# Attention and two MLPs on one core: the put-off product's matrices loaded two at a time into the token tile, and token loads, output stores and two late MLP1 products placed elsewhere

## The chip, the cores and the metric

The kernel runs on one NeuronCore of a Trainium2 chip. Its engines are TensorE (PE in the rows, its weight loads PEld), VectorE (DVE), ScalarE (ACT), GpSimd (POOL) and SyncE (SP), which here does nothing but issue DMAs. The metric is device time in microseconds of one execution; lower is better. The time of a kernel is the median of its runs, and a verdict of faster or slower is given beyond 2%.

## The reference

```python
def reference(...):                       # 4 x 8 heads, 768 positions, head size 64
    for c in range(24):                   # chunks of 32 queries
        # keys: 8 memory keys + positions c*32-16 .. c*32+40
        scores = q_c @ k_full.T / 8
        attn_out[c] = softmax(scores) @ v_full
    x = attn_out as 3072 tokens x 512
    h = x @ moe_w_in;  x = (h * sigmoid(h)) @ moe_w_out       # MLP1, 512 -> 2048 -> 512
    h = x @ moe2_w_in; r = max(h, 0); out = (r * r) @ moe2_w_out   # MLP2, same sizes
```

Everything is float32. The kernel splits an operand of a product into a high part and a remainder (`fp32r` tiles) and makes three matmuls for one.

## The kernel before, in words

**Stages.** Attention and MLP1 run first, in 6 blocks of 512 tokens. MLP1 (`mlp`, L745) takes 16 hidden tiles of a block: 12 matmuls of 128x512 into a hidden tile (L756 to L758), activation and split on ACT and DVE, then 12 matmuls (L790 to L792) that add the hidden tile's part to four output tiles `acc`. The result y1 is stored in DRAM (L831, L836). From about 612 us on MLP2 runs alone (`second`, L1203).

**MLP2.** Its two matrix products are made by a scheme of 2x2 blocks with 7 products in place of 8 (as Winograd's), on sums of blocks, called forms here. There are 6 blocks of 512 tokens, and in each 8 pairs of hidden tiles (k0 to k7). For a pair PE makes 7 "visits" (`visit`, L942: the sums of the tokens times the forms of the first weight matrix, tile `pp`) and 6 back products (`back_out`, `multiply` L1071: the squared hidden sums g times the forms of the second weight matrix, tile `out`). The back products lag: those of pair n stand among the visits of pairs n+1 and n+2. One such product is six matmuls of 128x256. The seventh back product of each pair is **put off**: its left operand stays in a `kept` tile, and the block's eight put-off products (`fourth`, here F0 to F7) are made among the visits of pairs k1 and k2 of the next block, those of the last block at the end. In a block there are so 8 x 13 + 8 = 112 products.

**What is loaded.** All forms of the second matrix (`w2s` in DRAM) are loaded anew in every block, by DMAs that SP issues at L1016: per pair one of 512 KB for back products 0 and 1 (here "f0"), two of 256 KB for 2 and 3 ("f2", "f3"), one of 512 KB for 4 and 5 ("f4"). The 512 KB ones use a ring of two buffers `wraw`, the 256 KB ones a ring of four buffers `wu`, which also take the eight 256 KB loads of the put-off products' forms (`load_fourth`). A load into a ring waits until PE is done with the buffer's last user. `tokens` (L849) reads a block's y1 back by four loads of 256 KB into a tile `xf` (L863), makes four differences of them (L875, on DVE or POOL), and splits seven forms (high part L900 on ACT, remainder L904 on DVE or POOL). xf and the last four splits live in a ring of two buffers "x", which MLP1 used before. Here a **border** is the stretch in which the next block's first pairs run: pair k0, and k1 and k2 with F0 to F7.

**Behind the put-off products.** `combine` adds the block's sums; three of its four output quarters are complete before F7 and are stored by `store` (L1180); `finish` adds the fourth and stores it.

**Order.** Each operation is a `Piece` with engines and costs, a due time and what it must follow. `Graph.order` plays the costs through on a model clock: an engine that is free takes the ready piece with the earliest due time. What comes out is each engine's program, which the chip then runs in that order; an engine that waits holds up all that stands behind it. SP's program is one such order, its DMAs go to one hardware queue, and at most eight are open at a time, since eight semaphores rotate. PE's products of MLP2 are chained in the order of the code (`on_tensor`).

Of the kernel before, what the change touches and what calls it, by code (L numbers as in the profile page):

```python
# [14 lines left out]
F32R = mybir.dt.float32r  # L15
# [173 lines left out]
def chunk_attention_two_mlps(ctx, tc, units, weights, out):  # L189
# [14 lines left out]
    for tag, n in (  # L204
        ("raw", 3), ("pr", 1), ("pts", 1), ("xq", 3), ("x", 2), ("g", 3), ("wraw", 2),
        ("wu", 4), ("wr", 4), ("nm", 3), ("sm", 4),
    ):
        pool(tag, n)
# [6 lines left out]
    def f(ap):  # L215
        return ap.bitcast(F32)
# [14 lines left out]

    ones, dense = G.buf("x"), G.buf("ph")

# [226 lines left out]
    def split_x(j, p, po, done, due):  # L460

        new = []
        if j not in x_buf:
            x_buf[j] = G.buf("x")
            x_done[j] = []
            new = [x_buf[j]]
        xb = x_buf[j]

        def x_high(e):
            if new:  # L470
                take(xb, [P, 2, KT, TB], F32R)
            nc.scalar.copy(xb.tile[:, 0, p, :], po.tile)

        def x_low(e):
            t = xb.tile
            nc.vector.tensor_tensor(t[:, 1, p, :], po.tile, f(t[:, 0, p, :]), op=ALU.subtract)

        a = G.add({"ACT": 0.64}, due - 1, x_high, [*done, *x_done[j]], new=new, uses=[po, xb])
        x_done[j].append(G.add({"DVE": 0.7}, due, x_low, [a], uses=[po, xb],
                               port=j >= ON_PE))  # L480
# [264 lines left out]
    def mlp(j):  # L745
        accs, earlier = None, []
        size = step_due(j, 1) - step_due(j, 0)
        for i in range(FT):
            ph, g, due = G.buf("ph"), G.buf("g"), step_due(j, i)
            wb, xb = w_buf[i], x_buf[j]  # L750
# [32 lines left out]
            def back(e, i=i, wb=wb, g=g, some=range(KT)):  # L783
                w, t = wb.tile, g.tile
                first, last = i == 0, i == FT - 1
                for m in some:
                    acc = accs[m]
                    o = take(acc, [P, TB], F32) if first else acc.tile
                    ws = slice(DM + m * P, DM + (m + 1) * P)
                    nc.tensor.matmul(o, w[:, 1, ws], t[:, 0], start=first, stop=False)  # L790
                    nc.tensor.matmul(o, w[:, 0, ws], t[:, 1], start=False, stop=False)  # L791
                    nc.tensor.matmul(o, w[:, 0, ws], t[:, 0], start=False, stop=last)  # L792

            if j == NB - 1 and i == FT - 1:
                break
            y = G.add({"PE": 2.8}, due + 2.4 * size, back, [d, w_done[i, 1]],
# [12 lines left out]

        def part(at, m):  # L810
            ys.append(on_tensor(MM, at, lambda e: back(e, some=[m]), [d, w_done[FT - 1, 1]], [],
                                [wb, g, accs[m]]))
            if m == KT - 1:
                store(ys)

        return y, [lambda at, m=m: part(at, m) for m in range(KT)]

# [31 lines left out]
    def tokens(b, due):  # L849

        t0 = b * T2
        after, xf = stored[b], G.buf("x")
        loads = []
# [4 lines left out]
        for n, (k, half) in enumerate(((0, 0), (2, 0), (2, 1), (0, 1))):  # L858
            def load(e, n=n, k=k, half=half):
                if n == 0:  # L860
                    take(xf, [P, 7, 2, HALF2], F32, "xf")
                at = t0 + half * HALF2
                nc.sync.dma_start(  # L863
                    out=xf.tile[:, n],
                    in_=y1[k:k + 2, :, at:at + HALF2].rearrange("k p t -> p k t"),
                )

            p = G.add({"SP": 0.45}, due - 50 + n, load, after, new=[xf] * (n == 0),
                      uses=[xf] * (n > 0), size=P * T2 * 4)
            p.behind += loads[:1]  # L870
            loads.append(p)

        def sums(o, a, b, after, at):
            def emit(e):
                engine[e].tensor_tensor(form(o), form(a), form(b), op=ALU.subtract)  # L875

            return G.add({"DVE": 0.72, "POOL": 1.35}, at, emit, after, uses=[xf], port=True)

# [8 lines left out]
        for rank, n in enumerate(X_FORM[p] for p in PRODUCTS):  # L887
# [3 lines left out]
            if shared:  # L891
                four = four or [G.buf("x")]
                x = four[0]
            else:
                x = G.buf("raw")
# [203 lines left out]

    def load_fourth(some, tag, due):  # L1100
        k, m = some[0].k, len(some)
        w, d = load_out(w2s[k:k + m, NF - 1], m, tag, due, [x for q in some for x in w2_kept[q.k]])
        for i, q in enumerate(some):
            q.fourth = (w, i, d)

    def load_pair(q, due, past=()):

        load_some(q, 0, 2, "wraw", due - 10)
        for k in range(4 if past else 0):
            load_fourth(past[k:k + 1], "wu", due - 11 + k)  # L1110
        for j in (2, 3):
            load_some(q, j, 1, "wu", due - 9 + j + (2 if past else 0))
        if past:
            for k in range(4, PAIRS):
                load_fourth(past[k:k + 1], "wu", due - 8 + k)
        load_some(q, 4, 2, "wraw", due - 5)
# [26 lines left out]
    def combine(b, due):  # L1143
# [24 lines left out]
        d12 = add(u2, 3, u2, [a4], 3)  # L1168
        store(b, y22, 1, 1, d22, due + 3)
        store(b, t1, 0, 0, d11, due + 4)  # L1170
        store(b, u2, 0, 1, d12, due + 5)
        return u3, [a4, d22]

    def store(b, y, half, side, after, due, m=None):
        r0, cs = b * T2 + half * HALF2, slice(side * HALF2, (side + 1) * HALF2)

        def emit(e):
# [3 lines left out]
            else:  # L1181
                nc.sync.dma_start(out=out[r0 + m * P:r0 + (m + 1) * P, cs], in_=y.tile[:, m])

        G.add({"SP": 0.45}, due, emit, [after], uses=[y],
              size=P * HALF2 * 4 * (2 if m is None else 1))

    def finish(b, u3, after, due):

        bank = banks[b, 4]
        for m, one in enumerate(bank):  # L1190
            def emit(e, m=m, one=one):
                if len(bank) == 1:
                    nc.vector.tensor_tensor(u3.tile, one.tile, u3.tile, op=ALU.add)
                else:
# [4 lines left out]
                      uses=[one, u3])  # L1199
            store(b, u3, 1, 0, d, due, None if len(bank) == 1 else m)  # L1200

    pairs = {}

    def second(rest):
        t, steps, xs, result = T20, NB2 * PAIRS, {}, {}
        half = PAIRS // 2
        for n in range(steps):
            q = pairs[n] = Pair(n)
            if q.k == 0:
                xs[q.b] = tokens(q.b, t)  # L1210
            one, two = pairs.get(n - 1), pairs.get(n - 2)
            past = [pairs[(q.b - 1) * PAIRS + k] for k in range(PAIRS)] if q.b else []
            if one:
                load_pair(one, t + 8 * MM, past if q.k == 1 else ())

# [12 lines left out]
            slots = [[x for x in some if not isinstance(x, tuple) or x[0]] for some in slots]  # L1228
            if n == 0:
                for i, x in enumerate(rest):  # L1230
                    slots[i].append(x)
            due, at = [], t
# [23 lines left out]
        past = [pairs[b * PAIRS + k] for k in range(PAIRS)]  # L1256
        for k in range(half):
            load_fourth(past[k:k + 1], "wu", t - 8 + MM * k)
        load_pair(one, t + 7 * MM)
        for k in range(half, PAIRS):  # L1260
            load_fourth(past[k:k + 1], "wu", t + MM * k)
        for k in range(half // 2, half):
# [7 lines left out]
        for j in range(NF - 1):  # L1270
            back_out(one, j, t)
            t += MM
        u3, after = combine(b, t)
        for x in past[half:]:
            fourth(x, t, True)
            t += MM
        finish(b, u3, after, t)

# [89 lines left out]
```

## Time and profile before

| | us |
|---|---|
| median of 3 runs | 1117.77 (1114.66 to 1492.04) |
| profiled execution | 1117.68 |
| its span, first to last instruction | 1115.8 |
| PE busy in the span | 1089.7 (98%) |
| DVE, ACT, POOL busy | 806.9, 517.3, 182.0 |

The profiled execution is an ordinary one: its time is that of the median. PE's busy time includes matmuls that run at the lower clock level and those that are drawn out behind a pause, so what the kernel could win is more than the idle 2%. The page's row of PE clocks has full speed (9 tenths or more) in 39 of 40 slices; slices are 28 us wide.

### The profile page before, as it was taken

To read this page: it belongs to the slowest core of one execution; us is meant where nothing else is said; L and a number is where in the kernel's file an instruction comes from. 1 tells how busy PE (TensorE), PEld (TensorE's weight loads), DVE (VectorE), ACT (ScalarE), POOL (GpSimd) and SP (SyncE) were. 2 spreads that over 40 slices of the span, in tenths; PEclk is the share of its full clock that TensorE was granted. 3 is DMA by queue.
4 is the path that set the end of the run, shared out by engine and by line. 5 is a ranking of instruction groups with operands and counts; after the bars stand their busy time and mean duration, and the time that the engine had idled before them with its cause. 6 is when DMAs were issued, how large, how long until landed. Compare 5 with 4: busy or idle time off the path is not lost.

```text
span 1115.8 us, 23506 instructions
## 1 busy us (share of the span) xinstructions
PE 1089.7 (98%) x9484; PEld 957.5 (86%) x9484; DVE 806.9 (72%) x1818; ACT 517.3 (46%) x926; POOL 182.0 (16%) x171
## 2 busy tenths in 40 slices
PE   7999999999999999999999999999999999999998
PEld 5677777777777777777888999899999999999997
DVE  4777777768778767775687767767767768768666
ACT  2888643544434444542566335334334335335332
POOL 0032202202101200110001202302302302303000
PEclk6999999999999999999999999999999999999999
DMA  7875344343334432431343556756756766755756
GB/s 267 274 231 181 105 139 163 117 143 114 118 129 157 149 123 96 143 128 39 120 134 127 158 170 190 245 171 181 255 171 199 244 171 206 244 164 174 234 170 206
DMA packets 94587, 188.36 MB, mean 169 GB/s; under 512 B 8464, under 2 KB 20752, under 8 KB 94480
## 3 DMA queue, kind: packets, MB, share of 16 engines
q1 hardware_dynamic: 94480, 186.88, 52.2%
q8 instruction: 74, 1.21, 0.5%
q14 instruction: 33, 0.27, 0.1%
HBM read 159.58 MB, written 27.26 MB: 167 GB/s over the span
## 4 chain that ended last, share of the span: by engine, by line
PE 92%; DMA 5%; issue 1%; SPq 1%; POOL 0%; DVE 0%; ACT 0%; POOLq 0%
PE pp L942 20%; PE out L1071 20%; PE ph L756 9%; PE ph L758 8%; PE acc L790 8%; PE ph L757 8%; PE acc L792 8%; PE acc L791 8%; DMA w<-w2s 3%; PE po L417 2%; PE sc L331 2%; DMA xf<-y 1%; PE turned L382 1%; DMA raw<-units 1%; DMA w<-weights 1%
## 5 line engine op out<-in xcount | busy, mean ns | idle before, releaser
L1071 PE MATMUL out<-w,g 128*128 128x256 f32 x2016 | 275.6, 284 | 11.5 <-DMA w<-w2s 10.4
L942 PE MATMUL pp<-xs,forms 128*128 128x256 f32 x2016 | 272.3, 281 | 0.5 <-ACT sums L959 0.5
L1071 PEld LDWEIGHTS out<-w,g 128*128 128x128 f32 x2016 | 255.7, 192 | 13.6 <-DMA w<-w2s 9.0
L942 PEld LDWEIGHTS pp<-xs,forms 128*128 128x128 f32 x2016 | 253.7, 189 | 1.6 <-ACT sums L959 1.1
L756 PE MATMUL ph<-x,w 128*128 128x512 f32 x384 | 156.7, 408 | 2.4 <-DVE w L572 1.7
L790 PE MATMUL acc<-g,w 128*128 128x512 f32 x384 | 153.2, 399 | 0.1
L758 PE MATMUL ph<-x,w 128*128 128x512 f32 x384 | 152.6, 397 | 0.0
L792 PE MATMUL acc<-g,w 128*128 128x512 f32 x384 | 152.1, 396 | 0.0
L1004 DVE TENSOR_TENSOR g<-sums,g 128x512 fp32r<-128x512 f32 x132 | 104.3, 790 | 65.4 <-ACT g L1000 65.4
L757 PE MATMUL ph<-x,w 128*128 128x512 f32 x384 | 151.5, 395 | 0.0
L791 PE MATMUL acc<-g,w 128*128 128x512 f32 x384 | 151.0, 393 | 0.0
L959 ACT ACTIVATE sums<-pp 128x256 f32<-128x256 f32 x192 | 74.0, 386 | 159.1 <-PE pp L942 127.6
L1000 ACT CAST g<-sums 128x512 fp32r<-128x512 f32 x144 | 89.3, 620 | 120.0 <-PE out L1071 116.3
L764 ACT ACTIVATE ph<-ph 128x512 f32<-128x512 f32 x96 | 55.9, 582 | 184.7 <-PE ph L758 181.5
L771 DVE TENSOR_TENSOR g<-ph,g 128x512 fp32r<-128x512 f32 x96 | 66.1, 689 | 47.2 <-ACT g L768 46.3
L391 DVE STREAM_TRANSPOSE turned<-pr 32x128 f32<-32x128 f32 x256 | 77.5, 303 | 26.7 <-ACT pr L402 22.1
L978 DVE SCALAR_TENSOR_TENSOR sums<-sums 128x256 f32<-128x256 f32 x144 | 65.8, 466 | 35.2 <-ACT sums L959 33.0
L756 PEld LDWEIGHTS ph<-x,w 128*128 128x128 f32 x384 | 72.4, 189 | 21.8 <-DVE w L572 2.4
L758 PEld LDWEIGHTS ph<-x,w 128*128 128x128 f32 x384 | 72.4, 189 | 17.8
L792 PEld LDWEIGHTS acc<-g,w 128*128 128x128 f32 x384 | 72.1, 188 | 17.7
L790 PEld LDWEIGHTS acc<-g,w 128*128 128x128 f32 x384 | 72.1, 188 | 17.2 <-DVE w L572 0.2
L791 PEld LDWEIGHTS acc<-g,w 128*128 128x128 f32 x384 | 72.1, 188 | 17.1
(89 smaller groups left out, 1234.1 us busy)
## 6 DMA issues: line engine op xcount, KB each, us to landing
w<-w2s SPq DMA_DIRECT2D x96, 512.0 KB, 3.9
w<-w2s SPq DMA_DIRECT2D x144, 256.0 KB, 3.2
wraw<-weights SPq DMA_DIRECT2D x40, 512.0 KB, 4.8
raw<-units SPq DMA_DIRECT2D x48, 384.0 KB, 4.3
w2s<-ws SPq DMA_DIRECT2D x56, 256.0 KB, 2.3
raw<-units SPq DMA_DIRECT2D x48, 260.0 KB, 4.8
w<-weights SPq DMA_DIRECT2D x24, 512.0 KB, 6.0
y<-y SPq DMA_DIRECT2D x24, 256.0 KB, 2.4
```

The costliest lines, as they stand in the source:

```text
L391: nc.vector.transpose(out=t[rs, :, cs], in_=src.tile[cs, :, rs])
L756: nc.tensor.matmul(o, w[:, 1, ws], x[:, 0, kt], start=(kt == 0), stop=False)
L757: nc.tensor.matmul(o, w[:, 0, ws], x[:, 1, kt], start=False, stop=False)
L758: nc.tensor.matmul(o, w[:, 0, ws], x[:, 0, kt], start=False, stop=(kt == KT - 1))
L790: nc.tensor.matmul(o, w[:, 1, ws], t[:, 0], start=first, stop=False)
L791: nc.tensor.matmul(o, w[:, 0, ws], t[:, 1], start=False, stop=False)
L792: nc.tensor.matmul(o, w[:, 0, ws], t[:, 0], start=False, stop=last)
L942: nc.tensor.matmul(o[:, at], w[:, a, ws], t[:, c, kt], start=first and kt == 0 and r == 0, stop=kt == 1 and r == 2, skip_group_check=True,)
L959: nc.scalar.activation(t[:, to], q.bank[bank].tile[:, h], func)
L1000: nc.scalar.copy(take(g, [P, 2, 2, HALF2], F32R, "g2")[:, :, 0], read())
L1004: engine[e].tensor_tensor(t[:, :, 1], read(), f(t[:, :, 0]), op=ALU.subtract)
L1071: nc.tensor.matmul(out_, g[:, at, a, gs], w[:, wat, c], start=first and r == 0 and (m == 0 or alone is not None), stop=last and r == 2, sk ...
```

## The change

The diff does five things.

- The ring "x" of two becomes two single buffers x0 and x1; xf always stands in x0, the four last splits in x1.
- The forms of a block's put-off products are loaded into x0, in xf's place, by four DMAs of 512 KB (two forms each, L1115 of the changed kernel) in place of eight of 256 KB into the ring `wu`. They are released as soon as the last split has read xf. The last block's four stand one in each of the last four pairs.
- The four loads of the next block's xf move from the border to the middle of the block before (due 50 us earlier, and not before that), the differences follow 10 us behind.
- The three early output quarters are stored behind the fourth, after F7.
- In MLP1's last block the hidden tiles are taken in the order 0 to 12, 14, 13, 15; the second products of 15 and of 13 are cut in four parts each, which stand in pair 0 (six) and pair 1 (two) of MLP2's first block; before only those of 15 were, in pair 0.

```diff
     for tag, n in (
-        ("raw", 3), ("pr", 1), ("pts", 1), ("xq", 3), ("x", 2), ("g", 3), ("wraw", 2),
+        ("raw", 3), ("pr", 1), ("pts", 1), ("xq", 3), ("x0", 1), ("x1", 1), ("g", 3), ("wraw", 2),
         ("wu", 4), ("wr", 4), ("nm", 3), ("sm", 4),
...
-    ones, dense = G.buf("x"), G.buf("ph")
+    ones, dense = G.buf("x1"), G.buf("ph")
...
         if j not in x_buf:
-            x_buf[j] = G.buf("x")
+            x_buf[j] = G.buf(f"x{j % 2}")
             x_done[j] = []
...
     def mlp(j):
-        accs, earlier = None, []
+        accs, earlier, parted = None, [], []
         size = step_due(j, 1) - step_due(j, 0)
-        for i in range(FT):
-            ph, g, due = G.buf("ph"), G.buf("g"), step_due(j, i)
+        late = (FT - 1, FT - 3) if j == NB - 1 else ()
+        row1 = [i for i in range(FT - 1) if i not in late] + [FT - 3] * bool(late) + [FT - 1]
+        end = late[-1] if late else FT - 1
+        for n, i in enumerate(row1):
+            ph, g, due = G.buf("ph"), G.buf("g"), step_due(j, n)
             wb, xb = w_buf[i], x_buf[j]
...
                 w, t = wb.tile, g.tile
-                first, last = i == 0, i == FT - 1
+                first, last = i == 0, i == end
                 for m in some:
...
-            if j == NB - 1 and i == FT - 1:
-                break
+            if i in late:
+                parted.insert(0, (i, wb, g, d, back))
+                continue
             y = G.add({"PE": 2.8}, due + 2.4 * size, back, [d, w_done[i, 1]],
...
-        def part(at, m):
-            ys.append(on_tensor(MM, at, lambda e: back(e, some=[m]), [d, w_done[FT - 1, 1]], [],
+        def part(at, m, i, wb, g, d, back):
+            ys.append(on_tensor(MM, at, lambda e: back(e, some=[m]), [d, w_done[i, 1]], [],
                                 [wb, g, accs[m]]))
-            if m == KT - 1:
-                store(ys)
-
-        return y, [lambda at, m=m: part(at, m) for m in range(KT)]
+            if m == KT - 1 and i == end:
+                store(ys[KT:])
+
+        return y, [lambda at, m=m, some=some: part(at, m, *some) for some in parted
+                   for m in range(KT)]
...
         t0 = b * T2
-        after, xf = stored[b], G.buf("x")
+        after, xf = stored[b], G.buf("x0")
         loads = []
...
             p.behind += loads[:1]
+            p.release = due - 50
             loads.append(p)
         def sums(o, a, b, after, at):
             def emit(e):
                 engine[e].tensor_tensor(form(o), form(a), form(b), op=ALU.subtract)
-            return G.add({"DVE": 0.72, "POOL": 1.35}, at, emit, after, uses=[xf], port=True)
+            p = G.add({"DVE": 0.72, "POOL": 1.35}, at, emit, after, uses=[xf], port=True)
+            p.release = due - 40
+            return p
...
             if shared:
-                four = four or [G.buf("x")]
+                four = four or [G.buf("x1")]
                 x = four[0]
...
-    def load_fourth(some, tag, due):
-        k, m = some[0].k, len(some)
-        w, d = load_out(w2s[k:k + m, NF - 1], m, tag, due, [x for q in some for x in w2_kept[q.k]])
-        for i, q in enumerate(some):
-            q.fourth = (w, i, d)
-
-    def load_pair(q, due, past=()):
+    def load_fourth(b, k, due, after=()):
+
+        w = pairs[b * PAIRS].fourth[0] if k else G.buf("x0")
+
+        def emit(e):
+            if k == 0:
+                take(w, [P, PAIRS, 2, HALF2], F32R, "w2")
+            nc.sync.dma_start(
+                out=f(w.tile)[:, k:k + 2],
+                in_=w2s[k:k + 2, NF - 1].rearrange("f p a c -> p f a c"),
+            )
+
+        d = G.add({"SP": 0.45}, due + k, emit, [*after, *w2_kept[k], *w2_kept[k + 1]],
+                  new=[] if k else [w], uses=[w] if k else [], size=4 * P * HALF2 * 4)
+        if k:
+            d.behind.append(pairs[b * PAIRS].fourth[2])
+        for i in range(2):
+            pairs[b * PAIRS + k + i].fourth = (w, k + i, d)
+
+    def load_pair(q, due):
         load_some(q, 0, 2, "wraw", due - 10)
-        for k in range(4 if past else 0):
-            load_fourth(past[k:k + 1], "wu", due - 11 + k)
         for j in (2, 3):
-            load_some(q, j, 1, "wu", due - 9 + j + (2 if past else 0))
-        if past:
-            for k in range(4, PAIRS):
-                load_fourth(past[k:k + 1], "wu", due - 8 + k)
+            load_some(q, j, 1, "wu", due - 9 + j)
         load_some(q, 4, 2, "wraw", due - 5)
...
         d12 = add(u2, 3, u2, [a4], 3)
-        store(b, y22, 1, 1, d22, due + 3)
-        store(b, t1, 0, 0, d11, due + 4)
-        store(b, u2, 0, 1, d12, due + 5)
-        return u3, [a4, d22]
-
-    def store(b, y, half, side, after, due, m=None):
+        leave = [(y22, 1, 1, d22), (t1, 0, 0, d11), (u2, 0, 1, d12)]
+        return u3, [a4, d22], leave
+
+    def store(b, y, half, side, due, after, m=None):
         r0, cs = b * T2 + half * HALF2, slice(side * HALF2, (side + 1) * HALF2)
...
-        G.add({"SP": 0.45}, due, emit, [after], uses=[y],
+        G.add({"SP": 0.45}, due, emit, after, uses=[y],
               size=P * HALF2 * 4 * (2 if m is None else 1))
-    def finish(b, u3, after, due):
+    def finish(b, u3, after, leave, due):
...
                       uses=[one, u3])
-            store(b, u3, 1, 0, d, due, None if len(bank) == 1 else m)
+            store(b, u3, 1, 0, due, [d], None if len(bank) == 1 else m)
+        if len(bank) == 1:
+            for n, (*what, d) in enumerate(leave):
+                store(b, *what, due + 2 + n, [d, banks[b, 4, "done"]])
...
                 xs[q.b] = tokens(q.b, t)
+                if q.b:
+                    for k in range(0, PAIRS, 2):
+                        load_fourth(q.b - 1, k, t + 2)
             one, two = pairs.get(n - 1), pairs.get(n - 2)
             past = [pairs[(q.b - 1) * PAIRS + k] for k in range(PAIRS)] if q.b else []
             if one:
-                load_pair(one, t + 8 * MM, past if q.k == 1 else ())
+                load_pair(one, t + 8 * MM)
+            if n >= steps - half:
+                load_fourth(q.b, 2 * (n - steps + half), t, row[-1:])
...
             slots = [[x for x in some if not isinstance(x, tuple) or x[0]] for some in slots]
-            if n == 0:
-                for i, x in enumerate(rest):
-                    slots[i].append(x)
+            if n < 2:
+                for some, x in zip(slots[n:], rest[n * 6:n * 6 + 6]):
+                    some.append(x)
             due, at = [], t
...
         past = [pairs[b * PAIRS + k] for k in range(PAIRS)]
-        for k in range(half):
-            load_fourth(past[k:k + 1], "wu", t - 8 + MM * k)
         load_pair(one, t + 7 * MM)
-        for k in range(half, PAIRS):
-            load_fourth(past[k:k + 1], "wu", t + MM * k)
         for k in range(half // 2, half):
...
             t += MM
-        u3, after = combine(b, t)
+        u3, after, leave = combine(b, t)
+        for n, (*what, d) in enumerate(leave):
+            store(b, *what, t + 3 + n, [d])
         for x in past[half:]:
             fourth(x, t, True)
             t += MM
-        finish(b, u3, after, t)
+        finish(b, u3, after, leave, t)
```

The programs that come out differ in three places that matter below.

SP at the first border before: row 243 and 244 are the loads f4 of pair k7 and f0 of pair k0, 245 the next block's xf, 246 and 247 loads through `wu`, L1180 the output stores; the 256 KB rows (128x512) from 250 on are mostly F loads.

```order
L1016 DMA w2_7775<-w2s_148 128x2x512
L1016 DMA w2_7805<-w2s_148 128x2x512
L863 DMA xf_7816<-y1_147 128x2x256 x4
L1016 DMA w2_7840<-w2s_148 128x512
L1016 DMA w2_7874<-w2s_148 128x512
L1016 DMA w2_7906<-w2s_148 128x2x512
L1180 DMA out<-y_7903 128x2x256
L1016 DMA w2_7918<-w2s_148 128x512
L1016 DMA w2_7930<-w2s_148 128x512
L1180 DMA out<-y_7795 128x2x256
L1180 DMA out<-y_7838 128x2x256
L1016 DMA w2_7959<-w2s_148 128x2x512
```

In these rows F loads, stores and the loads of the next pairs take turns. The same place in the changed program; L1115 is the new F load, L1024 the old L1016, L1194 the old L1180.

```order
L1024 DMA w2_7775<-w2s_151 128x2x512
L1024 DMA w2_7804<-w2s_151 128x2x512
L1115 DMA w2_7808<-w2s_151 128x2x512 x4
L1024 DMA w2_7839<-w2s_151 128x512
L1024 DMA w2_7874<-w2s_151 128x512
L1024 DMA w2_7904<-w2s_151 128x2x512
L1024 DMA w2_7954<-w2s_151 128x2x512
L1024 DMA w2_7996<-w2s_151 128x512
L1024 DMA w2_8009<-w2s_151 128x512
L1194 DMA out<-y_7908 128x2x256
L1194 DMA out<-y_7792 128x2x256
L1194 DMA out<-y_7837 128x2x256
```

Four F loads of 512 KB stand where the four xf loads of 256 KB stood, the eight F loads of 256 KB behind them are gone, and the stores stand together further back.

SP in the middle of the block, at pair 4, in the changed program; the row ahead of L868 (the old L863) is f4 of pair k3, the row behind it f0 of pair k4.

```order
L1024 DMA w2_8261<-w2s_151 128x512
L1024 DMA w2_8301<-w2s_151 128x512
L1024 DMA w2_8324<-w2s_151 128x2x512
L868 DMA xf_8328<-y1_150 128x2x256 x4
L1024 DMA w2_8356<-w2s_151 128x2x512
L1024 DMA w2_8380<-w2s_151 128x512
```

Before, nothing but L1016 rows stood there; 1 MB now stands between two loads of the pairs' forms.

POOL at the first border before: L904 and L875 belong to the tokens, L1004 is the remainder of a g that back products wait for.

```order
L904 TENSOR_TENSOR xs_7698<-xf_6832,xs_7698 128x512
L1004 TENSOR_TENSOR g2_7807<-kept_6898,g2_7807 128x2x256
L1004 TENSOR_TENSOR g2_7876<-sums_7728,g2_7876 128x2x256
L875 TENSOR_TENSOR xf_7816<-xf_7816 128x512
L1004 TENSOR_TENSOR g2_7908<-kept_7098,g2_7908 128x2x256
L875 TENSOR_TENSOR xf_7816<-xf_7816 128x512 x3
```

Here the differences stand between two g remainders. The same place in the changed program (L912 is the old L904, L1012 the old L1004, L993 a sum of hidden parts).

```order
L912 TENSOR_TENSOR xs_7606<-xf_7305,xs_7606 128x512
L912 TENSOR_TENSOR xs_7641<-xf_7305,xs_7641 128x512
L912 TENSOR_TENSOR xs_7700<-xf_7305,xs_7700 128x512 x2
L1012 TENSOR_TENSOR g2_7827<-sums_7604,g2_7827 128x2x256
L1012 TENSOR_TENSOR g2_7841<-kept_6866,g2_7841 128x2x256
L993 TENSOR_TENSOR sums_7728<-sums_7728 128x256
L1012 TENSOR_TENSOR g2_7879<-sums_7728,g2_7879 128x2x256
```

The differences of xf (L875) no longer stand among the g rows; POOL has more of the splits ahead of them (four here, three at each later border, one before).

## Rows read from the trace of the kernel before

**Rows 1.** Waits of PE, whole kernel: line, waited for, total us, times, longest.
```profile
PE out L1071 <- DMA w<-w2s: 10.4, 8, 2.7
PE out L1071 <- POOL g L1004: 0.9, 2, 0.5
PE pp L942 <- ACT sums L959: 0.5, 1, 0.5
```

**Rows 2.** Windows: stretch, length, busy us (x instructions) by engine, PE clock, DMA share, GB/s.
```profile
700.00:720.00 20.00, 17.26 (x134) 17.05 (x133) 13.52 (x23) 6.28 (x12) 6.99 (x6) 0.91 0.71 239
720.00:785.00 65.00, 65.00 (x549) 65.00 (x548) 47.70 (x97) 26.91 (x57) 12.48 (x12) 1.00 0.63 189
```

**Rows 3.** Chain of waits, undisturbed stretch: start, length, what; the same place of two pairs.
```profile
651.12 1.44 PE out L1071 x12
660.39 1.44 PE out L1071 x12
```

**Rows 4.** Timeline of PE: first visits of blocks 2 to 6, start and length.
```profile
684.50 2.29 PE L942 MATMUL pp<-xs,forms 128*128 128x256 f32 x18
768.86 2.29 PE L942 MATMUL pp<-xs,forms 128*128 128x256 f32 x18
851.13 2.29 PE L942 MATMUL pp<-xs,forms 128*128 128x256 f32 x18
933.38 2.29 PE L942 MATMUL pp<-xs,forms 128*128 128x256 f32 x18
1015.02 2.29 PE L942 MATMUL pp<-xs,forms 128*128 128x256 f32 x18
```

**Rows 5.** Timeline of PE: its last matmuls.
```profile
1106.18 5.99 PE L1071 MATMUL out<-w,g 128*128 128x256 f32 x48 [1.44 <-DMA w<-w2s]
```

**Rows 6.** Chain of waits at the first border.
```profile
703.25 6.95 DMA w<-w2s
...
710.25 2.93 PE out L1071 x12
713.17 1.62 PE pp L942 x12
```

**Rows 7.** Chain of waits at the third border.
```profile
860.40 6.15 DMA xf<-y
...
867.95 1.75 POOL g L1004
...
876.21 1.70 PE out L1071 x12
```

**Rows 8.** Timeline of SP at the first border: start, length, issues.
```profile
694.34 4.99 SPq L1016 DMA_DIRECT2D w<-w2s  x3
...
702.54 9.71 SPq L1016 DMA_DIRECT2D w<-w2s  x6
```

**Rows 9.** Line L863, first border, loads 1 and 2, then 3 and 4.
```profile
L863 SPq DMA_DIRECT2D xf<-y x2: 409/434/460, 692.3 to 692.8; - x2
DMA to landing us min/median/max: 4.6/4.7/4.8
...
L863 SPq DMA_DIRECT2D xf<-y x2: 462/466/469, 693.3 to 693.8; - x2
DMA to landing us min/median/max: 5.0/5.1/5.3
```

**Rows 10.** Line L1016, 720 to 785 us: its loads' time to landing.
```profile
DMA to landing us min/median/max: 2.5/3.6/5.3
```

**Rows 11.** Splits of tokens, both engines: count, busy us, mean ns, idle before.
```profile
L904 POOL TENSOR_TENSOR xs<-xf,xs 128x512 fp32r<-128x512 f32 x6 | 10.0, 1664 | 10.9 <-ACT xs L900 10.9
L904 DVE TENSOR_TENSOR xs<-xf,xs 128x512 fp32r<-128x512 f32 x36 | 32.6, 917 | 3.8 <-ACT xs L900 3.8
```

**Rows 12.** Timeline of POOL and DVE at the first border: the last splits there.
```profile
688.45 1.74 POOL L904 TENSOR_TENSOR xs<-xf,xs 128x512 fp32r<-128x512 f32 x1
688.96 1.78 DVE L904 TENSOR_TENSOR xs<-xf,xs 128x512 fp32r<-128x512 f32 x1
```

## Prediction

> **What bounds the kernel now.** I read the table of PE's waits first, because PE is busy for 98% of the span and only what PE waits for can be won. In MLP2 it waits 10.4 us for loads of `w2s` in eight waits, 0.9 us for a remainder g that POOL makes in two, and once 0.5 us for ACT [rows 1]; together 11.8 us. The reader should look at where they lie: the windows show PE busy for all 65.00 us of the stretch 720 to 785, the undisturbed middle of a block, and for 17.26 of 20 us at the first border, with a mean clock of 0.91 [rows 2].
>
> A wait costs more than its length, so I next measured each block as a whole. In the undisturbed stretch a pair takes 660.39 - 651.12 = 9.27 us [rows 3], that is 0.713 us for each of its 13 products. A block has 8 x 13 + 8 = 112 products: 8 x 9.27 + 8 x 0.713 = 79.9 us. The first visits of blocks 2 to 6 stand at 684.50, 768.86, 851.13, 933.38 and 1015.02 [rows 4], which gives 84.4, 82.3, 82.2 and 81.6 us: 4.5, 2.4, 2.4 and 1.8 us too many. From the last of them to the end of the last matmul, 1106.18 + 5.99 = 1112.17 [rows 5], are 97.15 us. There PE makes 56 visits, 48 back products of the block, 9 left from the block before and 16 put-off ones: 129 products, 92.0 us. The displayed start of a group overlaps the group before by about 0.16, so 5.0 are too many. Sum: **16.1 us** lost in MLP2's borders and tail, against 11.3 us of waits of the back products. The chain shows the rest: after a pause twelve matmuls take 1.70 us [rows 7] instead of 1.44 [rows 3], 0.26 for each of ten waits; and after the longest, 2.7 us, the first twelve took 2.93 and the next 1.62 [rows 6], about 1.7 us above the pace, at a lowered clock.
>
> **Why the loads are late at a border.** The chain at the first border ends in a load of 256 KB issued at 703.25 that took 6.95 us to land [rows 6], where loads of the same line in the undisturbed stretch take 2.5 to 5.3, median 3.6 [rows 10]. SP issues four xf loads from 692.3 on [rows 9], three loads through 699.3, and the loads of F4 to F7 only from 702.54 [rows 8]: in the program they stand behind xf, behind stores, and through a ring of four buffers behind PE's use of F0 and on. So the F loads start late and then share the queue with everything else.
>
> **The change part by part.**
>
> *F loads and xf loads at the border.* The four new F loads stand where the xf loads stood, released by the last split, and wait for no F product. They carry 2 MB where xf had 1 MB; the eight single F loads behind, 2 MB, go, so the border carries 1 MB less. The xf loads landed at 692.3 + 4.6 = 696.9, 692.8 + 4.8 = 697.6, and, the fourth, 693.8 + 5.3 = 699.1 [rows 9]: 0.73 us for 256 KB. F0 and F1 (512 KB) should land when the second xf load did, 697.6. PE needs F0 after 20 products, 684.66 + 14.3 = 698.9: 1.3 us early. F2 and F3 land at about 699.1 and are needed 5 products later than F0, at 702.5; F4 to F7 at 700.6 and 702.0, needed at 707.5 and later. The pairs' own loads behind come up to 2.9 us later than now; f4 of k0 lands eleven such pieces behind the first, 704.9; it is issued, and so its buffer free, at about 699 [rows 8], and a load is needed 10 us after that (worked out below), so 4 us early. So the waits for DMA go in all four inner borders and the one in the last block, with the pace after them. I take all 16.1 us as the upper end of the gain.
>
> *The xf loads in mid block.* They stand between f4 of k3 and f0 of k4. PE needs f0 of k4 84 matmuls after it releases the buffer of f4 of k3, 84 x 0.119 = 10.0 us. In that time the queue moves 512 KB, 1 MB and 512 KB. By the border's rows the fourth xf load lands 699.1 - 692.3 = 6.8 us after the first issue [rows 9] (0.5 behind the release), and 512 KB more take 1.5: 8.8 us, 1.2 us early. The nearest bad row is the third border, where the fourth xf load was issued at 860.40 and took 6.15 us [rows 7]; the first issue being 1.5 earlier, as in [rows 9], 7.6 in place of 6.8 gives 9.6 us, still 0.4 early. I take no cost, and the misses of the rivals as the upper bound.
>
> *Differences and splits.* In the row of the chain at the third border POOL's g is late, and ahead of it in the chain is the landing of xf [rows 7]: POOL had to do the differences first. In the change they are in mid block, DVE takes 18 of 24 (5 before), and POOL takes 17 of 42 splits (6 before). A split takes 1664 ns on POOL, 917 on DVE [rows 11]. The last splits at the first border ended at 690.2 and 690.7 [rows 12], the first F load is held until about 692.3 by the load ahead in the queue: 1.5 us of room. DVE and POOL are far from full (47.70 and 12.48 of 65 us [rows 2]); neither adds to the sum while this room holds. The Trainium skill, "SBUF — State Buffer" (section "SBUF: two separate sides"), speaks against the move: POOL and a DVE operation with two inputs in SBUF lock each other out of a shared port for a whole instruction. The two splits that overlap and take 1.74 and 1.78 us [rows 12] agree, the DVE mean being 917 ns; by that rule each split moved to POOL would also cost DVE up to its 1.66 us, which is what rival B would be made of, while the sum by the rows stays as it is.
>
> *Stores.* They move past the border's loads. SP waits for the last sum of the block with f4 of k1 queued behind, but that load waits for PE until about a microsecond (11 matmuls) later, so the stores cost nothing; if the sum came 3 us late, f4 of k1 would still have the slack of a normal load (10.0 less 3.6 us [rows 10]).
>
> *MLP1's last products.* Same matmuls in other places; visits begin 2.8 us earlier and so the first g is ready earlier relative to the work left. The wait of 0.5 us for ACT [rows 1] should go: gain 0.5 us, with nothing and 1 us as ends. y1 of the last block is stored later; it is read only four blocks on.
>
> **The sum** goes against the profiled execution, 1117.68 us, which is the median of the runs (1117.77). All gone: 1117.7 - 16.1 - 0.5 = 1101.1. I leave 2 us for what is late next: two waits of the POOL kind with their restarts, 2 x (0.45 + 0.26) = 1.4, and 0.6 for the first pair. **Forecast 1103 us**, chance 0.60.
>
> **Rivals.**
>
> *A. Mid-block loads a little late.* If the f0 load of k4 lands at 10.5 instead of 8.8 us after the release, each of five blocks pauses 0.5 us and restarts for 0.26: 3.8 us, about **1107**. For it: 1 MB in one piece on a single queue; against it: DMA share there is 0.63 [rows 2], so there is room. Chance 0.16. The Trainium skill, "DMA: Bandwidth & Descriptors" (section "Queues, rings and completion order"), says that a queue's descriptors are consumed in ring order on each DMA engine, which speaks for this rival: a load can't pass the 1 MB ahead of it. The rows agree, the xf loads landing in order of issue [rows 9].
>
> *B. F0 late at the borders.* With more splits on POOL, the last split ends later; from 1.5 us on it holds the F load, and 1.3 us more reach PE. One POOL split after another (four in row at the first border, 4 x 1.66 = 6.7 us) could do it; with 1 us of wait and 0.26 of restart in five places 6.3 us stay, **1109**. Against it: the splits start early, when the previous block's last visits release tiles. Chance 0.09.
>
> *C. The stall only moves.* If the border is limited by bytes and not by where the loads stand, some other load is late there: only POOL's waits and ACT's go, 0.9 + 2 x 0.26 + 0.5, **1116**. For it: 239 GB/s at the first border against 189 in mid block [rows 2]. Against it: 1 MB less goes through. Chance 0.10.
>
> *D. Slower.* The mid-block wait becomes like the worst border wait: 2.7 us, restart and lowered clock, 2.7 + 1.7 = 4.4 us [rows 1, 6], and the borders keep half their loss (8 us). Then 1103 + 5 x 4.4 + 8 - 2 = **1131**. It decides from 0.88 us per 256 KB on (8.8 - 8 x 0.73 = 3.0 to start, 3.0 + 8 x 0.88 = 10.0), and the wait is 2.7 at 1.2. No undisturbed load was that slow: 512 KB landed in 5.3 us at most [rows 10]. Chance 0.05.
>
> **Range and chances.** Forecast, A and B make 0.85, so the range goes from 1099.5, the floor of 1101.1 less what runs differ (the fastest was 0.3% below the median), to 1111, B with a little more. Two per cent, about what a measurement of this kernel can tell from no change, is 22 us: faster than 1095.4 lies beyond the floor, 0.03; slower than 1140 needs more than D, 0.02; the rest, 0.95, within.
>
> **What would show it.** Right: no PE wait for `w2s` above 0.3 us, block periods of 80 to 80.5 us, a clock of 1.00 at 700 to 720 us. A shows as waits of `out` on a `w2s` load at about 45 us into each block; B as waits for the load of L1115 with its issue well behind the load ahead; C as waits at the borders for L1024; D as both with a lowered clock. I am wrong if the median is above 1111, or if the waits go and the periods stay above 81 us.

## The result and the profile after

The changed kernel takes **1102.0 us** (median of 4 runs, 1100.71 to 1103.13) against 1117.47 before (median of 4: 1114.66 to 1117.77, and one of 1492.04). The ratio, which leaves out the run of 1492.04 us, is 0.987 with a 95% interval of 0.984 to 0.990: a gain of 1.3%, measured clearly, though inside the 2% of a verdict. The forecast was 1103 us, in a range of 1099.5 to 1111.

PE's table of waits (columns as in [rows 1]), its longest lines and the one of MLP2:

```profile
PE po L417 <- issue: 2.7, 1, 2.7
PE ph L759 <- DVE w L572: 2.2, 1, 2.2
...
PE out L1079 <- DMA w<-w2s: 0.2, 1, 0.2
```

Of the 11.8 us in [rows 1] one wait of 0.2 is left in MLP2; all other waits in the table lie in the first 60 us, ahead of the part that the change is about. The windows say the same; the first border has lost its pause and its lowered clock [rows 2]:

```profile
700.00:720.00 20.00, 20.00 (x171) 20.00 (x170) 14.41 (x30) 7.17 (x14) 3.60 (x4) 1.00 0.75 231
720.00:785.00 65.00, 65.00 (x549) 65.00 (x548) 49.00 (x97) 27.88 (x58) 17.95 (x16) 1.00 0.68 216
```

PE's timeline, first visits of blocks 2 to 6, and the group that ends the program [rows 4, 5]:

```profile
685.86 2.29 PE L950 MATMUL pp<-xs,forms 128*128 128x256 f32 x18
765.77 2.29 PE L950 MATMUL pp<-xs,forms 128*128 128x256 f32 x18
845.69 2.29 PE L950 MATMUL pp<-xs,forms 128*128 128x256 f32 x18
925.60 2.29 PE L950 MATMUL pp<-xs,forms 128*128 128x256 f32 x18
1005.51 2.29 PE L950 MATMUL pp<-xs,forms 128*128 128x256 f32 x18
...
1084.71 13.12 PE L1079 MATMUL out<-w,g 128*128 128x256 f32 x108
```

Every period is 79.91 or 79.92 us, which is 112 products of 0.713: blocks 2 to 5 run at PE's pace without a break. From the last of these visits to the end of the last matmul, 1084.71 + 13.12 = 1097.83, are 92.3 us (97.15 before).

SP's timeline at the first border [rows 8], and what line L1115 reports for the first F load and for all four (columns as in [rows 9]):

```profile
691.03 2.52 SPq L1024 DMA_DIRECT2D w<-w2s  x2
693.65 1.95 SPq L1115 DMA_DIRECT2D w<-w2s  x4
695.71 12.81 SPq L1024 DMA_DIRECT2D w<-w2s  x6
708.62 1.79 SPq L1194 DMA_DIRECT2D out<-y  x3
```

```profile
L1115 SPq DMA_DIRECT2D w<-w2s x1: 410/410/410, 693.7 to 693.7; - x1
DMA to landing us min/median/max: 5.1/5.1/5.1
...
L1115 SPq DMA_DIRECT2D w<-w2s x4: 410/462/476, 693.7 to 695.1; - x4
DMA to landing us min/median/max: 5.1/6.5/8.1
```

F0 and F1 landed at 693.7 + 5.1 = 698.8, 12.9 us into the block as forecast, and 1.3 us ahead of use. The last pair landed at 695.1 + 8.1 = 703.2: six pieces of 256 KB in 4.4 us, 0.73 each, the rate that the forecast took from xf.

The load of f0 of k4 in the first block, the one that PE waited for, by line L1024 and by PE's timeline:

```profile
L1024 SPq DMA_DIRECT2D w<-w2s x1: 413/413/413, 656.0 to 656.0; - x1
DMA to landing us min/median/max: 7.6/7.6/7.6
```

```profile
663.63 1.70 PE L1079 MATMUL out<-w,g 128*128 128x256 f32 x12 [0.20 <-DMA w<-w2s]
```

It landed 0.2 us after PE could have used it. In the four blocks after that it was 0.4 to 1.4 us early (landing against the first matmul that uses it).

**A measure for the experiments.** In their first hundred us the programs of all kernels here have the same rows, yet the 1000th matmul starts anywhere from 79.7 to 83.4 us in their profiles (80.6 before, 82.6 after): pauses and clock of the first 60 us differ from run to run. So beside times I give **M2**, the time from the start of the first back product to the end of the last matmul in the profile: before 625.29 to 1112.17, **486.9**; after 626.18 to 1097.83, **471.7**; 15.2 less.

M2 comes from one profile of each kernel, where the times are medians of several runs. With MLP1's order alone changed it is 485.9, 1.0 less than before, and single waits at the borders then differ by up to 1.3 us (2.7 and 1.4 us for F4 at the first border). So I read nothing from differences of about 1 us, and where M2 and the run times disagree both are given.

### The profile page after: what moved, and what is told of

Read it like the earlier page. It is cut to its first block, busy times and chain, and to the rows that moved or that the text cites. A ratio compares the mean times of both kernels' runs of the same rounds, so it can differ in the third digit from the quotient of the medians.

```text
span 1101.3 us, 23447 instructions
## 1 busy us (share of the span) xinstructions
PE 1085.9 (99%) x9484; PEld 955.9 (87%) x9484; DVE 795.7 (72%) x1808; ACT 515.6 (47%) x926; POOL 190.1 (17%) x181
## 4 chain that ended last, share of the span: by engine, by line
PE 96%; DMA 2%; ACT 1%; issue 0%; DVE 0%; POOL 0%; SPq 0%
PE out L1079 22%; PE pp L950 21%; PE ph L759 9%; PE ph L760 8%; PE ph L761 8%; PE acc L793 8%; PE acc L794 8%; PE acc L795 8%; PE po L417 2%; PE sc L331 2%; PE turned L382 1%; DMA w<-w2s 1%; DMA w<-weights 1%; DMA raw<-units 1%; ACT wu L493 0%
## 5 line engine op out<-in xcount | busy, mean ns | idle before, releaser
L1079 PE MATMUL out<-w,g 128*128 128x256 f32 x2016 | 272.8, 282 | 0.2 <-DMA w<-w2s 0.2
L1012 DVE TENSOR_TENSOR g<-sums,g 128x512 fp32r<-128x512 f32 x123 | 95.7, 782 | 57.4 <-ACT g L1008 56.0
L759 PEld LDWEIGHTS ph<-x,w 128*128 128x128 f32 x384 | 72.7, 189 | 23.2 <-DVE w L572 2.9
L761 PEld LDWEIGHTS ph<-x,w 128*128 128x128 f32 x384 | 72.8, 190 | 17.4
L760 PEld LDWEIGHTS ph<-x,w 128*128 128x128 f32 x384 | 72.9, 190 | 15.9
```

The lines of the kernel that those rows point to most:

```text
L759: nc.tensor.matmul(o, w[:, 1, ws], x[:, 0, kt], start=(kt == 0), stop=False)
L760: nc.tensor.matmul(o, w[:, 0, ws], x[:, 1, kt], start=False, stop=False)
L761: nc.tensor.matmul(o, w[:, 0, ws], x[:, 0, kt], start=False, stop=(kt == KT - 1))
L1012: engine[e].tensor_tensor(t[:, :, 1], read(), f(t[:, :, 0]), op=ALU.subtract)
L1079: nc.tensor.matmul(out_, g[:, at, a, gs], w[:, wat, c], start=first and r == 0 and (m == 0 or alone is not None), stop=last and r == 2, sk ...
```

## The experiments

**The three parts, each alone in the kernel before.** First xf: the two release times of the diff, nothing else.

```diff
             p.behind += loads[:1]
+            p.release = due - 50
             loads.append(p)
...
+            p.release = due - 40
```

> The kernel before, with the xf loads alone released 50 us ahead of their block and the differences 40 us ahead, so that both stand in mid block; F loads through the ring of four, stores and MLP1 as before. Theory 1, as in the prediction (the F loads are late because xf and its 1 MB stand ahead of them): most of the waits for loads at the borders go, 10.4 us of them fall below 3, both POOL waits go; time about 1106. Theory 2 (by 698.95 us the queue had caught up with xf, a load issued then landed in 4.0 us; what delays F4 is what is issued from 699 to 704: three stores, two single loads of k0, f0 of k1, and the ring that holds F4 back): the POOL waits go, 0.9 and two restarts of 0.26, the DMA waits stay above 7 us; time 1113 to 1117.

Measured: ratio 1.002 (1.000 to 1.003), M2 485.5. PE's waits, and the chain at the first border:

```profile
PE out L1074 <- DMA w<-w2s: 11.2, 9, 2.5
PE pp L945 <- ACT sums L962: 1.1, 2, 0.6
```

```profile
704.17 6.69 DMA w<-w2s
710.86 0.04 issue
710.90 1.70 PE out L1074 x12
```

The POOL waits are gone; the waits for loads are not. With 1 MB less ahead of it the F4 load still takes 6.69 us (6.95 in [rows 6]). Theory 1 falls: xf was out of the way by the time F4 was asked for. And there is a second wait for ACT, of 0.6 us, in mid block, where the differences now stand; the section on why the prediction was right comes back to it.

Then the stores: `combine` and `finish` as in the diff.

> The kernel before, with the three early output stores put behind F7 as in the change, and nothing else. Theory 1: the stores' place matters little, the DMA waits stay above 8 us; time 1115 to 1118. Theory 2: F4 lands earlier by what the three stores took in the queue, 0.7 to 1.9 us each, some 3 us; the border waits of 2.7, 1.6, 1.3, 0.8 and 1.5 us shrink to below 0.5 each; only the wait in the tail (1.4) and those for POOL stay; DMA waits below 4 us; time 1107 to 1111.

Measured: ratio 0.994 (0.992 to 0.996), median 1110.1, M2 476.5. Waits, and the F4 load at the first border by line L1016:

```profile
PE out L1071 <- DMA w<-w2s: 2.4, 4, 1.5
PE out L1071 <- POOL g L1004: 0.7, 1, 0.7
PE pp L942 <- ACT sums L959: 0.5, 1, 0.5
```

```profile
L1016 SPq DMA_DIRECT2D w<-w2s x1: 320/320/320, 705.7 to 705.7; - x1
DMA to landing us min/median/max: 4.4/4.4/4.4
```

Theory 2 holds: F4 lands 4.4 us after its issue and not 6.95, and the waits for loads fall from 10.4 us to 2.4. How much of the whole gain that is, the two measures put differently: M2 falls by 10.4 of 15.2 us, two thirds, while the medians of whole runs fall by 6.4 us (1116.5 for the kernel before, measured beside it) of 15.5, two fifths. The two profiled runs themselves lie 8.1 us apart, the start of the second being 2.3 us longer (1000th matmul at 82.9 us after 80.6). How much of the 10.4 belongs to the runs that happened to be profiled is not shown.

One of the three left in its place (`store` for y22 in `combine`, the other two in `leave`):

> The kernel before with two of the three early output stores put behind F7; one, the first, stays among the border's loads (it stands ahead of two of k0's loads, the other two stood behind them). Theory bytes: each store of 256 KB ahead of F4 costs the loads behind it its share of the queue, 0.7 to 0.9 us; F4 then lands 1.5 us earlier than before and 0.8 later than with all three moved; DMA waits of PE about 5 us, between the 10.4 of before and the 2.4 measured with all three moved. A rival, that any store among the loads disturbs them as a whole: DMA waits stay above 8 us. A third, that only the stores behind k0's singles hurt: DMA waits at 2.4 us as with all moved.

Measured: 0.994 (0.991 to 0.996), median 1112.6, M2 479.1; in M2 7.8 us less than before and 2.6 more than with all three moved.

```profile
PE out L1071 <- DMA w<-w2s: 3.9, 5, 1.7
PE out L1071 <- POOL g L1004: 1.0, 2, 0.6
```

In waits and M2 it lies between the two as the theory of bytes says, 3.9 us of waits for loads where about 5 were expected. Whole runs don't tell it from all three moved: both are at 0.994.

MLP1's order and parts alone (`mlp` and the loop over `rest` as in the diff):

> The kernel before, with the new order of MLP1's last hidden tiles and their second products in eight parts, and nothing else. Both theories: the wait of 0.5 us for ACT at the start of MLP2 goes, all else stays; 0.5 to 1.0 us less, time 1116 to 1117. If the later y1 stores or the POOL chain ahead of the first back product mattered, a new wait of PE would stand near 626 us and the time would be that of before or more.

Measured: 0.9998 (0.998 to 1.002), too little to see among whole runs. In the profile the wait for ACT is gone, and from the 5400th matmul, in MLP1, to the first back product are 21.0 us where before there were 22.1: 1.0 us, the upper end of the forecast's 0 to 1. The DMA waits stay, 10.3 us.

**Stores and xf together**, F still through the ring of four:

> The kernel before with the stores behind F7 and the xf loads and differences in mid block; F loads still single, through the ring of four. Theory (stores and bytes ahead decide, the ring costs little by itself): the border waits left by the stores' move go too, DMA waits below 1 us, POOL's 0.7 gone, the 0.5 for ACT at the start of MLP2 stays; MLP2 within 1.5 us of the changed kernel, the time 1 to 3 us above it, 1103 to 1106. A rival (the ring holds F4 to F7 back, whatever stands ahead): DMA waits stay at 2 us or more and the time is that with the stores alone, about 1110.

Measured: 0.992 (0.989 to 0.994), median 1109.2, M2 476.4, as with the stores alone (476.5). DMA waits 3.3 us in five waits, longest 1.1. F4 at the first border, by line L1019 and by what SP waited for just then:

```profile
L1019 SPq DMA_DIRECT2D w<-w2s x1: 320/320/320, 705.0 to 705.0; - x1
DMA to landing us min/median/max: 4.5/4.5/4.5
...
SPq L1019 <- PE out L1074: 0.3, 1, 0.3
```

The rival holds: the last 4.8 us of M2 need F loads that don't wait for the ring. At the first border F4 was issued 18.75 us into the block in the kernel before and in those with xf, the stores or both moved, each time after a wait of SP for PE, whatever stood ahead. Only its landing changed: 6.95 us after the issue, 6.7 with xf moved, 4.4 with the stores moved, 4.5 with both. PE needs it 22.9 us into the block (32 products), so from this issue time even the shortest of the four comes a little late.

**The stores put back in the changed kernel** (`store` in `combine` again, nothing in `leave`):

> The changed kernel, with the three early output stores where they were before, among the border's loads. Both theories: the F loads are issued 5 to 10 us ahead of them, F0 keeps its 1.3 us or more and F4 its 5, so the time is that of the changed kernel, 1101 to 1103. A rival: f0 of k1, k1's singles or f4 of k1, now behind the stores, come late; then new waits of 0.5 to 1 us at each border and 1104 to 1108.

Measured: 0.989 (0.986 to 0.991), median 1102.8, M2 471.8, no wait of PE in MLP2. With F loaded early the stores' place is worth nothing.

**F4 to F7 late in the changed kernel**, with the stores behind F7 and ahead of them:

```diff
             d.behind.append(pairs[b * PAIRS].fourth[2])
+        if k >= PAIRS // 2 and not after:
+            d.release = due + 14.5
```

> The changed kernel with the loads of F4 to F7 released 16.5 us after the block's start at the four inner borders and the last one (due + 14.5 in the planner's clock), so that they stand behind f0 of k1, where F4 stood before; at the first border they fall behind k2's singles as well. Stores behind F7. Theory (F4 was late by its late issue and by what stands ahead of it in the queue, stores above all): at borders 2 to 5 the pair F4, F5 is issued at about 18.2 us into the block, with 512 KB ahead, lands 4.5 to 5.2 later and is needed at 22.9: waits of 0 to 0.5 us each; at the first border 2 to 4 us; DMA waits of PE in all 3 to 6 us, time 1105 to 1110.

> The same with the three early output stores back among the border's loads, now ahead of F4 to F7. Theory: 768 KB more ahead, 2.2 to 2.9 us, so waits of 2 to 3 us at each of borders 2 to 5 and somewhat more at the first; 10 to 15 us of DMA waits, time 1114 to 1120: the stall of before, built into the changed kernel. A rival (with the forms in x0 and not in the ring the stores do no harm, as with F loaded early): the same time as without the stores there, 1105 to 1110.

Measured: 0.996 (0.994 to 0.997) and 0.999 (0.998 to 1.001), medians 1112.2 (1105 to 1110 were expected) and 1115.7, M2 482.6 and 485.8. Waits of the first and of the second, and from the second's timeline the waits at borders 2 and 3:

```profile
PE out L1079 <- DMA w<-w2s: 7.2, 3, 6.8
```

```profile
PE out L1079 <- DMA w<-w2s: 9.5, 4, 5.1
...
796.64 1.70 PE L1079 MATMUL out<-w,g 128*128 128x256 f32 x12 [1.90 <-DMA w<-w2s]
878.84 1.70 PE L1079 MATMUL out<-w,g 128*128 128x256 f32 x12 [1.99 <-DMA w<-w2s]
```

The first border is a case apart, its loads being placed behind k2's; I had 2 to 4 us there and it was 6.8 and 5.1. At borders 2 to 5 the waits are 0.2, 0.2, 0 and 0 without and 1.9, 2.0, 0.6 and 0 with the stores ahead. So stores ahead of late F loads bring a stall back, in this kernel too, but 4.5 us over the four borders where 8 to 12 were expected.

**1 MB more in mid block** (the xf loads issued twice, into a tile of eight forms):

```diff
-        for n, (k, half) in enumerate(((0, 0), (2, 0), (2, 1), (0, 1))):
+        for n, (k, half) in enumerate(((0, 0), (2, 0), (2, 1), (0, 1)) * (2 if b else 1)):
```

> The changed kernel with each of the four xf loads of blocks 2 to 6 issued twice, the second time into three unused forms and one added one of the tile, so that 2 MB stand in mid block in place of 1; the differences wait for all. Theory (rival A of the prediction is a matter of bytes against a slack of 0 to 1.4 us): the 1 MB more takes 2.9 us in the queue, some of it ahead of the release, so the load of f0 of k4 or f4 of k3 is 0.5 to 1.5 us late in each of five blocks; with restarts 4 to 9 us, time 1106 to 1111. If the slack were larger than the measured landings say: no wait and 1102.

Measured: 0.997 (0.996 to 0.999), median 1114.7, M2 483.5, 11.8 us more than the changed kernel. Waits, and two windows with their clocks (columns as in [rows 2]):

```profile
PE out L1080 <- DMA w<-w2s: 9.5, 5, 2.7
...
665.68 1.69 PE L1080 MATMUL out<-w,g 128*128 128x256 f32 x12 [2.72 <-DMA w<-w2s]
```

```profile
655.00:675.00 20.00, 17.28 (x146) 17.08 (x145) 11.26 (x26) 5.45 (x12) 5.09 (x4) 1.00 0.80 261
735.00:755.00 20.00, 18.09 (x140) 17.88 (x139) 11.99 (x26) 5.57 (x12) 2.66 (x3) 0.91 0.75 251
```

Rival A's mechanism is real and was one megabyte away: five waits, of 1.3 to 2.7 us, longer than expected.

**The xf loads spread out** (`p.release = due - 50 + 2.15 * n`), which the late load in the first block suggested:

> The changed kernel with the four xf loads released 2.15 us apart, so that loads of the pairs stand between them. Theory: the one wait of 0.2 us in mid block goes and the slack of f0 of k4 grows from 0 to 1.4 us to 1.5 us or more; the time is that of the changed kernel less 0.2 to 0.5, not measurable: 1101 to 1102.5. A rival: the differences come later, and a split at the next border with them: new waits, above 1103.

Measured: 0.986 (0.983 to 0.988), median 1102.5, the same as the changed kernel. The wait for the load is gone, but three others, for DVE, have come:

```profile
PE pp L950 <- DVE kept L976: 0.5, 3, 0.2
```

M2 is 473.2, 1.5 us more. There is no gain in it.

**Eight F loads of 256 KB in place of four of 512** (one form in each `load_fourth`):

> The changed kernel with each F form loaded by a DMA of its own, eight of 256 KB in the place of four of 512 KB. Theory: place and bytes decide, not the size of one DMA; F0 lands 0.7 us earlier than the pair did, the rest as before; no new wait, 1101 to 1103. A rival (each DMA costs a time of its own, and no more than eight can be open, so the eight F loads hold up SP until the first have landed): the loads of the pairs behind are issued 2 to 3 us later, new waits of up to 1 us at each border, 1103 to 1108.

Measured: 0.988 (0.986 to 0.989), median 1103.4, M2 471.2, no wait in MLP2. The Trainium skill, "DMA: Bandwidth & Descriptors" (section "Bandwidth"), advises to batch DMAs to 1 MB or more; here halving them from 512 to 256 KB changed nothing that the profile shows. So it is not the size of the F loads that does the work.

## Why the prediction was right, and where its reasons were not

*The ceiling.* 16.1 us in borders and tail and 0.5 at the start of MLP2 were named as what could go. 15.2 and 1.0 went: nearly all. Measuring whole blocks against the undisturbed pace was worth more than adding up waits (11.8). Of the signs named, no wait above 0.3 us and a clock of 1.00 came; the periods, 79.9 us, are even a little under the 80 to 80.5.

*The 2 us left for what is late next* were not needed: one wait of 0.2 and its restart of 0.26. That the forecast of 1103 and the profiled 1103.04 agree is in part luck: the start took about 2 us longer in this profile than in that of before. The median of the runs lies 1 us below the forecast. The lower end of the range is not what its words give: 1101.1 less 0.3% is about 1098, not 1099.5; the fastest run took 1100.71.

*F loads at the border, xf in mid block.* Landing times came out within 0.2 us (698.8 and 703.2; 1.3 us of slack). In mid block a slack of 1.2 us, at worst 0.4, was worked out; it was 0.4 to 1.4 in four blocks, and 0.2 us too late in the first: right in size, with one block over the edge. The rival's price was taken too low; 1 MB more cost 11.8 us.

*Why the loads were late before* is the step that failed. The prediction named xf, the stores and the ring without a price for each, and its case against rival C was that 1 MB less goes through the border. Its sum rests on the early landing of the F loads, and that came out. The relief from xf's bytes did not: that MB, taken away alone, gave nothing: waits for loads 11.2 us after 10.4, run times the same. (M2 fell by 1.4. POOL's two waits and their restarts make that up; the clock, which here stayed at full at the first border, may have had a part.) F4 was late because the ring kept its issue until 18.75 us into the block, and because three stores stood ahead of it there. Moving the stores wins two fifths to two thirds of the gain; early F loads win all of it, stores or no stores. Moving xf makes room for F in x0. That "the stores cost nothing" is true of their new place in the changed kernel, and hid what they cost in their old one.

*POOL and DVE.* Both POOL waits went, as argued, and by xf's move alone. More splits on POOL did not reach PE in the changed kernel, and rival B did not come. The splits by line, both engines [rows 11]:

```profile
L912 POOL TENSOR_TENSOR xs<-xf,xs 128x512 fp32r<-128x512 f32 x17 | 25.7, 1512 | 58.2 <-ACT xs L908 58.2
L912 DVE TENSOR_TENSOR xs<-xf,xs 128x512 fp32r<-128x512 f32 x25 | 20.8, 841 | 0.2 <-ACT xs L908 0.2
```

They are shorter on average than before, not longer, but that does not mean that the two engines leave each other alone. In the changed kernel the 14 DVE splits during which POOL runs nothing take 0.68 to 0.69 us, and the 11 that overlap an operation of POOL take 1.04 on average and up to 1.78 (17 of 36 overlapped before). The differences of xf show the same, and there it has reached PE. With xf alone moved, the second wait for ACT goes back to one of them (the chain of waits, and the timelines of POOL and DVE):

```profile
823.53 1.70 DVE xf L876
825.23 1.50 DVE sums L988 x2
...
828.04 0.29 ACT sums L962
828.33 0.04 issue
828.37 0.98 PE pp L945 x6
...
823.27 3.10 POOL L876 TENSOR_TENSOR xf<-xf 128x512 f32<-128x512 f32 x2 [7.47 <-DVE xf L876]
823.45 1.79 DVE L876 TENSOR_TENSOR xf<-xf 128x512 f32<-128x512 f32 x1
```

A difference that takes DVE 0.68 us alone took 1.79 beside POOL's, the first sum behind it, also beside one of POOL's, 1.50 where such a sum takes 0.42 alone, and PE waited 0.6 us. Both kernels with late F loads have one such wait of 0.6 us in mid block too, with the same chain. The changed kernel has none: that the differences cost nothing came out, but three kernels close to it pay.

Rival C, the stall that only moves, is refuted by every window; what held it up, the higher GB/s at a border, is still there (231) without a stall.

What stays open: why the waits with the stores ahead fade from 2.0 us at border 3 to 0 at border 5 in the kernel with late F loads, and how much of the old stall the stores alone were, between M2's two thirds and the run times' two fifths.

## What to carry to other kernels

A load that is late has three causes to be told apart: what it waited for before its issue, what stood ahead of it in its queue at that moment, and its own length. Read the issue time first; work that was queued long before (xf, 10 us earlier) may already be through. Stores that nobody waits for belong behind the loads that somebody does, or the loads must be issued early enough not to care. And one profile of each kernel is not enough to price a part: put its difference beside that of the run times.

## What the runs showed of the hardware that was not expected

The clock of TensorE did not follow the length of a wait. After a wait of 2.74 us before, and of 1.91 in the kernel with 2 MB in mid block, the granted clock fell to its lower level (means of 0.91 in 20 us); after waits of 2.72 us in that same kernel and of 2.48 with xf moved alone it stayed at 1.00, and the first twelve matmuls took 1.69 and 1.70 us where those after the 2.74 took 2.93 [rows 6]. The window of the kernel with xf moved alone (columns as in [rows 2]):

```profile
700.00:720.00 20.00, 17.52 (x147) 17.31 (x146) 13.46 (x25) 6.77 (x13) 2.61 (x2) 1.00 0.75 249
```

The 1.7 us that the prediction put down to the longest wait were thus no fixed price.
